# Attention and mixture of experts in one kernel: zero products in the opening, key copies by heads, three weight halves on GpSimd, first tokens in the scores' banks

## The chip, the cores and the metric

The kernel runs on one core of a Trainium2 chip. The metric is the time of one execution in device microseconds (us). The core's engines work side by side and meet through semaphores: TensorE (PE in the profile: matrix products and transposes), VectorE (DVE), ScalarE (ACT), GpSimd (POOL) and SyncE (SP), which issues most DMAs. TensorE writes its results to PSUM, eight banks of 128 x 512 fp32; ScalarE and VectorE read them from there.

## The reference

Block-sparse attention over 4 batches of 8 heads, then a mixture of 16 experts (4 groups of 4) with one expert for each of the 3072 tokens. Cut to what matters:

```python
# attention: S=768, D=64, blocks of 32 keys, window 16
k_sum = k.reshape(B, H, nb, block, D).max(axis=3)
v_sum = v.reshape(B, H, nb, block, D).mean(axis=3)
scores_l = scale * np.matmul(q, k.transpose(0, 1, 3, 2))     # kept where |i - j| < 16
scores_s = scale * np.einsum('bhsd,bhnd->bhsn', q, k_sum) + np.log(block)
a = softmax(concat([where(mask_l, scores_l, -1e9), scores_s]))
x = (a @ concat([v, v_sum])).transpose(0, 2, 1, 3).reshape(B * S, H * D)
# experts: N=3072, D=512, G=4, Eg=4, F=1024
g_idx, g_w = argmax and softmax weight of x @ w_group
e_idx, e_w = argmax and softmax weight of xg @ w_expert[g]
h = np.maximum(xg[mask_e] @ w1[g, e], 0.0)
out[tok_idx] = (g_w * e_w)[:, None] * (h @ w2[g, e])
```

## The kernel before

**Attention.** The 32 heads are done in 16 pairs, each in three steps (g = 0, 1, 2 of query rows). What a step does, and in which order, stands in the table `PLAN`; `START` is the same for the first four steps. The letters: `s` the score products into the scores' banks, `e` VectorE's masked maxima (tiles ss, nm) and ScalarE's exponentials (pr), `t` their transposes, `v` the product with the values and VectorE's division (rs, xt), `m` the block means of the values, `l` the router's logits, `p0` to `p4` the preparation of the next pair. `p0` and `p1` are `put_k` for head 0 and head 1 of the pair: TensorE transposes the head's keys into a bank of `ps_tr` (three banks, in turn), and two copies of 64 rows each, j = 0 and j = 1, put them into the tile kw. `p2` and `p3` do the queries (qt, on ScalarE), and `p4` copies the pads inside kw, takes the block maxima (ks) and copies them in (VectorE). `w` issues four products of zeros (`keep_warm(4)`, 128 x 512 bf16), whose result nobody reads.

**Hand-over.** The function `hook` is called after each step. Around the last ones it begins with the expert that has the most blocks of tokens, called "first": `gather1` fetches two blocks of its tokens (xg) by an indirect DMA from GpSimd, `x_t1` transposes them and splits them into a high and a low half (xT), and `split_w` splits a quarter of the weights w1: ScalarE rounds the high half (w1h), VectorE subtracts it from the weights for the low half (w1l). Products of both halves together have the precision wanted, three for each pair of operands.

**The first expert.** It has four blocks of 128 tokens, done two at a time. Stage 1 (`stage1_2`) makes the hidden layer in four half-blocks jj, 24 products each, each into one bank of the scores; ScalarE then takes the positive part (hTh) and VectorE the low half of that (hTl). During the first pass w2 is split in four parts (w2h, w2l). Stage 2 multiplies with w2. Then come the units (two blocks, one block or small ones) of all experts, one after the other, up to the end.

**Order.** It is fixed when the program is built: each engine executes its instructions in program order. The router's VectorE operations are interleaved by a planner (`Clock`), which sums up estimated times of TensorE and VectorE and puts in router work where VectorE is ahead. Banks are handed out by a ring for each kind (`Banks.next`): "tr" has three banks (63 to 65 in the orders below), "s" three (66 to 68), "av" one (69) and "lg" one (70). When the attention's last steps are built, the third bank of "s" is taken out of its ring and given to "av"; by then two half-blocks of stage 1 have been built.

Of the kernel before, what the change touches and what calls it, by code (L numbers as in the profile page):

```python
# [20 lines left out]
P = 128  # L21
# [29 lines left out]
        ["s", "p3", "l3", "t", "v", "l0", "m0", "e"]]  # L51
START = [["s", "e"], ["s", "m0", "e"], ["s", "w", "t", "m1", "p0", "p1", "e", "p4", "p2", "p3"],
         ["t", "v", "s", "n0", "p0", "p1", "e", "p4"]]
LAG = {"l0": 1, "l1": 2, "l2": 2, "l3": 2}
# [13 lines left out]

XT_AT = 4


# [18 lines left out]
class Clock:  # L90

    pe, dve = float("-inf"), 0.0
    step = 0
# [496 lines left out]
def attention(tc, q, k, v, w_group, w_expert, ident, x_dram, ps, router, hook):  # L590
# [24 lines left out]
    with ExitStack() as st, ExitStack() as nat_st:  # L615
# [125 lines left out]
        def prep(idx, part):  # L741
# [18 lines left out]
            def put_k(h):  # L760
                rows = slice(64 * h, 64 * h + 64)
                out = kw[rows, :, 0:QT].rearrange("p t (r i j) -> p j t r i", i=4, j=2)
                for j, tv in enumerate(tr(kn, h)):
                    (nc.scalar.copy if j == 0 or h and idx in ACT_K1 else V.tensor_copy)(  # L764
                        out=out[:, j], in_=tv.rearrange("p i t r -> p t r i"))
# [121 lines left out]
        for n in range(NG + 3):  # L887
# [4 lines left out]
            for step in START[n] if n < len(START) else PLAN[g]:  # L892
# [10 lines left out]
                elif step[0] == "m" and n < NG:  # L903
                    j = idx + (step == "m0" and n > 2)
                    if (j > 0 or n < 3) and j < len(order):
                        means(j, int(step[1]))
                elif step == "w":
                    keep_warm(4)
                elif step == "n0":
# [36 lines left out]
class Experts:  # L946
# [76 lines left out]
    def split_w(self, row, which, parts, low=True, high=True):  # L1023

        raw = self.raw(row, which)
        for c in parts:
# [9 lines left out]
            if low:  # L1036
                self.V.tensor_tensor(out=l, in0=src, in1=h.bitcast(F32), op=ALU.subtract)

# [7 lines left out]

    def split_t(self, cols, hi, lo, b):

        nc = self.nc
        tp = self.bank("tr", b).rearrange("p (c t) -> p c t", c=4)  # L1050
        for c in range(4):
# [42 lines left out]

    def x_t(self, x, i):
        hi, lo = self.parts(i)
        for half in range(2):
            self.split_t(lambda c: x[half][:, c * P:(c + 1) * P], hi[:, :, half], lo[:, :, half], half)

# [166 lines left out]

    def x_t1(self):
        self.x_t(self.xg1, 0)

# [70 lines left out]
def block_attention_then_moe(tc, q, k, v, w_group, w_expert, w1, w2, out):  # L1340
    nc = tc.nc
    with ExitStack() as st:
# [16 lines left out]
        def hook(n, need, advance, space):  # L1359
# [7 lines left out]
            if n == last - GATHER_AT:  # L1367
                need(2)
                ex.gather1(0)
                ex.load_w(("first", 0), 1, queue=nc.gpsimd)  # L1370
            if n == last - X_AT:
                ex.x_t1()
                if NE > 2:
                    ex.gather1(2)
            for part in range(4):
                if n == last + SPLIT_AT[part] + 1:
                    ex.split_w(("first", 0), 0, [part], high=False)
                if n == last + SPLIT_AT[part]:
# [70 lines left out]
```

## Time and profile before

| | |
|---|---|
| time, median of 3 runs | 515.81 us (514.64 to 517.34) |
| time of the profiled execution | 515.85 us |
| its span, first to last instruction | 514.2 us |
| mean granted TensorE clock | 0.986 |
| TensorE busy | 492.2 us (96%) |
| VectorE busy | 356.6 us (69%) |
| ScalarE busy | 317.8 us (62%) |
| GpSimd busy | 120.9 us (24%) |

The profile is that of one execution. Busy shares are averages over stages with different limits: attention to about 171 us, the first expert to about 236 us, and the units behind it. The granted clock is a share of TensorE's full 2.4 GHz; 0.50 is 1.2 GHz. What ended an engine's idle time stands behind an arrow in the rows, as in "0.45 <-DVE kw".

### The profile page before, as it was taken

How to read it: one execution, taken by the hardware profiler on the slowest of the kernel's cores; microseconds unless marked ns; L12 is line 12 of the kernel's file. 1: busy time of each engine (PE TensorE's matmuls, PEld its weight loads, DVE VectorE, ACT ScalarE, POOL GpSimd, SP SyncE). 2: the span in 40 equal slices, each digit the busy share in tenths (PEclk: the TensorE clock that was granted, in tenths of full speed). 3: DMA queues.
4: the chain of work that ended last, by engine and by line, in shares of the span. 5: the costliest groups of instructions: out<-in, count | busy, mean ns of one | idle time of the engine just before them, and what ended most of it. 6: DMA issues, size and time to landing. Idle time of an engine off the chain costs nothing.

```text
span 514.2 us, 13346 instructions
## 1 busy us (share of the span) xinstructions
PE 492.2 (96%) x4974; PEld 415.5 (81%) x4974; DVE 356.6 (69%) x1084; ACT 317.8 (62%) x597; POOL 120.9 (24%) x205
## 2 busy tenths in 40 slices
PE   8999999999999899999999999999999999999994
PEld 4677767776777698979898989898898989897773
DVE  6687899888977978878755647483836556473773
ACT  5699888888988643216644556473645546474682
POOL 6122112211312600037020203022121202022332
PEclk9799999999999899999999999999999999999998
DMA  9999676879646820069997665665566756754891
GB/s 179 176 181 198 130 168 189 180 155 195 173 113 224 281 90 22 28 220 354 409 403 273 238 229 211 247 225 190 205 211 239 263 212 222 258 191 137 300 359 42
DMA packets 75316, 106.94 MB, mean 208 GB/s; under 512 B 40286, under 2 KB 40366, under 8 KB 75232
## 3 DMA queue, kind: packets, MB, share of 16 engines
q1 hardware_dynamic: 69184, 86.78, 58.5%
q0 software_dynamic: 6048, 19.12, 10.4%
q8 instruction: 43, 0.70, 0.6%
q14 instruction: 41, 0.34, 0.2%
HBM read 97.49 MB, written 13.24 MB: 215 GB/s over the span
## 4 chain that ended last, share of the span: by engine, by line
PE 49%; issue 19%; DMA 12%; DVE 11%; ACT 3%; POOL 3%; POOLq 1%; DVEq 0%; ACTq 0%
PE ps_s L122 26%; DMA out_dram<-y,t_unit_scatter 12%; PE ps_tr L122 12%; PE ps_av L122 10%; DVE ss L795 3%; DVE ks L775 2%; DVE kw L764 1%; ACT kw L764 1%; PE ps_lg L122 1%; POOL ohr L1042 1%; ACT qt L758 1%; PE ps_lg L662 1%; POOLq L1185 1%; ACT pr L804 1%; DVE kw L778 1%
## 5 line engine op out<-in xcount | busy, mean ns | idle before, releaser
L122 DVE TENSOR_TENSOR w2l<-w2r,w2h 128x1024 fp32r<-128x1024 f32 x52 | 63.4, 1225 | 77.1 <-ACT w2h L1035 76.6
L122 PE MATMUL ps_s<-xT,w1h 128*128 128x256 f32 x448 | 83.5, 284 | 0.0
L122 PEld LDWEIGHTS ps_s<-xT,w1h 128*128 128x128 f32 x448 | 70.7, 192 | 1.0 <-issue 0.7
L1082 POOL DMA_INDIRECT out_dram<-y,t_unit_scatter x24 | 25.7, 1069 | 190.9 <-ACT y L1077 97.7
L738 POOL COPY va<-vr 25x256 f32<-25x256 f32 x96 | 35.9, 418 | 118.8 <-DVE vr L735 118.8
L122 PE MATMUL ps_s<-xT,w1l 128*128 128x256 f32 x224 | 63.4, 283 | 0.0
L122 DVE TENSOR_TENSOR w1l<-w1r,w1h 128x1024 fp32r<-128x1024 f32 x52 | 60.4, 1219 | 3.6 <-ACT w1h L1035 3.6
L804 ACT ACTIVATE pr<-ss,nm 128x120 f32<-128x120 f32 x192 | 60.1, 387 | 3.3 <-DVE nm L795 2.9
L1120 ACT ACTIVATE hTh<-ps_s 128x512 fp32r<-128x512 f32 x48 | 28.7, 598 | 53.9 <-PE ps_s L122 31.9
L122 PE MATMUL ps_s<-ohr,w1h 128*128 128x256 f32 x320 | 58.9, 282 | 0.0
L1035 ACT CAST w2h<-w2r 128x1024 fp32r<-128x1024 f32 x52 | 53.8, 1041 | 1.5 <-DVE lg L865 0.9
L1035 ACT CAST w1h<-w1r 128x1024 fp32r<-128x1024 f32 x52 | 50.7, 1051 | 0.4 <-DMA w1r<-in_moe_w_dram 0.4
L122 PEld LDWEIGHTS ps_s<-ohr,w1h 128*128 128x128 f32 x320 | 49.8, 188 | 0.2
L122 DVE SCALAR_TENSOR_TENSOR hTl<-ps_s,hTh 128x512 fp32r<-128x512 f32 x48 | 33.2, 691 | 24.2 <-ACT hTh L1120 21.5
L795 DVE CUSTOM_DVE_ANT_0 ss<-mask,ps_s 128x120 f32<-128x120 f32 x192 | 42.1, 275 | 6.1 <-PE ps_s L122 4.6
L122 PE MATMUL ps_s<-ohr,w1l 128*128 128x256 f32 x160 | 45.0, 281 | 0.0
L122 PEld LDWEIGHTS ps_s<-xT,w1l 128*128 128x128 f32 x224 | 42.9, 192 | 0.3
L122 PE MATMUL ps_s<-kw,qt 64*64 64x120 f32 x768 | 37.5, 282 | 5.7 <-DVE nm L795 4.6
L122 PE MATMUL ps_s<-w2h,hTh 128*128 128x512 f32 x104 | 41.6, 400 | 0.0
L122 PE MATMUL ps_av<-w2h,hTh 128*128 128x512 f32 x104 | 41.6, 400 | 0.0
L122 PE MATMUL ps_av<-w2l,hTh 128*128 128x512 f32 x104 | 41.1, 395 | 0.0
L122 PE MATMUL ps_s<-w2h,hTl 128*128 128x512 f32 x104 | 41.1, 395 | 0.0
(275 smaller groups left out, 1010.6 us busy)
## 6 DMA issues: line engine op xcount, KB each, us to landing
w1r<-in_moe_w_dram SPq DMA_DIRECT2D x30, 1024.0 KB, 8.4
w2r<-in_moe_w_dram SPq DMA_DIRECT2D x28, 1024.0 KB, 5.6
kn<-in_k_dram SPq DMA_DIRECT2D x16, 384.0 KB, 4.5
qn<-in_q_dram SPq DMA_DIRECT2D x16, 384.0 KB, 5.4
va<-in_v_dram SPq DMA_DIRECT2D x32, 192.0 KB, 5.0
x_dram<-xt SPq DMA_DIRECT2D x12, 512.0 KB, 5.4
w2r<-in_moe_w_dram POOLq DMA_DIRECT2D x4, 1024.0 KB
va<-in_v_dram SPq DMA_DIRECT2D x64, 44.0 KB, 4.6
```

The source lines that it names most:

```text
L122: return f(*args, **kw)
L662: nc.tensor.matmul(out=t, lhsT=zero, rhs=zero[:, None, :].broadcast_to([P, 4, P]), start=True, stop=True)
L738: nc.gpsimd.tensor_copy(out=va[KW:NR, i:i + n, :, 0:D], in_=vr[KW:NR].broadcast_to([NBLK + 1, n, 2, D]))
L758: nc.scalar.activation(out=out[:, j], in_=tv.rearrange("p i t r -> p t i r"), func=AF.Copy, scale=-1.0 / 8.0)
L764: (nc.scalar.copy if j == 0 or h and idx in ACT_K1 else V.tensor_copy)(out=out[:, j], in_=tv.rearrange("p i t r -> p t r i"))
L775: V.reduce_max(out=ks, axis=AX.X, in_=kw[:, :, 0:QT].rearrange("p t (a k) -> p t a k", k=BLOCK))
L778: V.tensor_copy(out=kw[:, :, KW:NC], in_=ks[:, None, :].broadcast_to([P, NQT, NBLK]))
L795: V.tensor_tensor_reduce(out=ss[:, u], in0=mask[:, 1 if t == 0 else 2 if t == NQT - 2 else 0], in1=sp[h][:, j], scale=1.0, scalar=3.4e38, ...
L804: nc.scalar.activation(out=pr[:, i, 0:NC], in_=sp[:, i], func=AF.Exp, bias=nm[:, i:i + 1], scale=-1.0)
L1035: self.nc.scalar.copy(out=h, in_=src)
L1082: self.nc.gpsimd.indirect_dma_start(out=self.out, out_offset=bass.IndirectOffsetOnAxis(ap=self.tabs[name, "scatter"][0:y.shape[0], col:col ...
L1120: nc.scalar.activation(out=th[:, js], in_=hp, func=AF.Relu)
```

## The change

It has five parts. (1) The opening's `w` is written `w4`, and two more places issue zero products: `w2` ahead of p3 in step 2 and `w3` ahead of the scores in step 3. (2) `put_k` gives both copies of head 0 to ScalarE and both of head 1 to VectorE, where before each head's first copy went to ScalarE and its second to VectorE. For pairs from 10 on (`ACT_K1`), ScalarE had both copies of head 1; now it has that head's first. (3) Of the first expert's eight low halves three are subtracted by GpSimd: part 2 of w1, parts 1 and 3 of w2. (4) The first token transposes (`x_t1` in `hook`) take banks of "s" instead of "tr". (5) In `hook` the low halves are built ahead of `x_t1` and of the second `gather1`.

```diff
-START = [["s", "e"], ["s", "m0", "e"], ["s", "w", "t", "m1", "p0", "p1", "e", "p4", "p2", "p3"],
-         ["t", "v", "s", "n0", "p0", "p1", "e", "p4"]]
+START = [["s", "e"], ["s", "m0", "e"], ["s", "w4", "t", "m1", "p0", "p1", "e", "p4", "p2", "w2", "p3"],
+         ["t", "v", "w3", "s", "n0", "p0", "p1", "e", "p4"]]
...
+LOW_BY_POOL = ((0, 2), (1, 1), (1, 3))
...
                 for j, tv in enumerate(tr(kn, h)):
-                    (nc.scalar.copy if j == 0 or h and idx in ACT_K1 else V.tensor_copy)(
+                    (nc.scalar.copy if h == 0 or j == 0 and idx in ACT_K1 else V.tensor_copy)(
                         out=out[:, j], in_=tv.rearrange("p i t r -> p t r i"))
...
             if low:
-                self.V.tensor_tensor(out=l, in0=src, in1=h.bitcast(F32), op=ALU.subtract)
+                self.low(row, which, c).tensor_tensor(out=l, in0=src, in1=h.bitcast(F32), op=ALU.subtract)
+
+    def low(self, row, which, c):
+        return self.nc.gpsimd if row[0] == "first" and (which, c) in LOW_BY_POOL else self.V
...
-    def split_t(self, cols, hi, lo, b):
+    def split_t(self, cols, hi, lo, b, bank="tr"):
 
         nc = self.nc
-        tp = self.bank("tr", b).rearrange("p (c t) -> p c t", c=4)
+        tp = self.bank(bank, b).rearrange("p (c t) -> p c t", c=4)
...
+            for part in range(4):
+                if n == last + SPLIT_AT[part] + 1:
+                    ex.split_w(("first", 0), 0, [part], high=False)
             if n == last - X_AT:
-                ex.x_t1()
+                ex.x_t1("s")
                 if NE > 2:
                     ex.gather1(2)
             for part in range(4):
-                if n == last + SPLIT_AT[part] + 1:
-                    ex.split_w(("first", 0), 0, [part], high=False)
                 if n == last + SPLIT_AT[part]:
                     ex.split_w(("first", 0), 0, [part], low=False)
```

What stands in a row of VectorE in the middle of the attention, between the maxima of one step and the pads of kw, before:

```order
L764 COPY kw_135<-ps_tr_63 64x12x32
L848 COPY xT<-ps_tr_64 128x256
L826 RECIPROCAL rs<-ps_av_69 128x4
L827 TENSOR_TENSOR xt_113<-ps_av_69,rs 128x2x128
L764 COPY kw_135<-ps_tr_63 64x12x32
L772 COPY kw_135<-kw_135 128x11x16
```

and of the changed kernel, at the same place (its lines from 762 on are counted one higher):

```order
L849 COPY xT<-ps_tr_64 128x256
L827 RECIPROCAL rs<-ps_av_69 128x4
L828 TENSOR_TENSOR xt_113<-ps_av_69,rs 128x2x128
L765 COPY kw_135<-ps_tr_63 64x12x32 x2
L773 COPY kw_135<-kw_135 128x11x16
```

The copy of head 0 that stood ahead of the division by rs is gone from here, and two copies of head 1 stand behind it.

ScalarE in stage 1 of the first expert's first pass; `hTh` is the positive part of a half-block, read from the bank named behind the arrow. Before (the fourth reads ps_s_67):

```order
L1120 ACTIVATE hTh_3102<-ps_s_66 128x512
L848 COPY xT<-ps_tr_65 128x256
L861 COPY lT<-ps_lg_70 128x192
L1120 ACTIVATE hTh_3102<-ps_s_67 128x512
L1035 CAST w2h_3483<-w2r_3096 128x1024 x2
L1120 ACTIVATE hTh_3102<-ps_s_66 128x512
```

and now:

```order
L1124 ACTIVATE hTh_3107<-ps_s_68 128x512
L849 COPY xT<-ps_tr_63 128x256
L862 COPY lT<-ps_lg_70 128x192
L1124 ACTIVATE hTh_3107<-ps_s_66 128x512
L1036 CAST w2h_3488<-w2r_3101 128x1024 x2
L1124 ACTIVATE hTh_3107<-ps_s_66 128x512
L1036 CAST w2h_3488<-w2r_3101 128x1024 x2
L1124 ACTIVATE hTh_3107<-ps_s_67 128x512
```

The second and the third half-block, jj = 1 and 2, now use the same bank, 66; VectorE's hTl read the same banks in the same order.

TensorE behind the last product of stage 1 of the second pass, where stage 2 of the third block begins; `ps_lg<-ohr,bo_unit` are products that build the table of the units' tokens. Before:

```order
L122 MATMUL ps_av_69<-w2h_3483,hTh_3102 128x512
L122 MATMUL ps_av_69<-w2l_3484,hTh_3102 128x512
L122 MATMUL ps_av_69<-w2h_3483,hTl_3103 128x512
L122 MATMUL ps_av_69<-w2h_3483,hTh_3102 128x512
L122 MATMUL ps_av_69<-w2l_3484,hTh_3102 128x512
L122 MATMUL ps_av_69<-w2h_3483,hTl_3103 128x512
L122 MATMUL ps_lg_70<-ohr,bo_unit 62x128 x6
```

and now:

```order
L123 MATMUL ps_lg_70<-ohr,bo_unit 62x128 x18
L123 MATMUL ps_av_69<-w2h_3488,hTh_3107 128x512
L123 MATMUL ps_av_69<-w2l_3489,hTh_3107 128x512
L123 MATMUL ps_av_69<-w2h_3488,hTl_3108 128x512
L123 MATMUL ps_av_69<-w2h_3488,hTh_3107 128x512
L123 MATMUL ps_av_69<-w2l_3489,hTh_3107 128x512
L123 MATMUL ps_av_69<-w2h_3488,hTl_3108 128x512
L123 MATMUL ps_lg_70<-ohr,bo_unit 62x128 x6
```

18 of the 24 products moved ahead of stage 2, and six behind its first six; before, the other 18 came six matmuls later. The 24 products of `bo_unit` with ohr that follow, behind one product of the look-up (ps_lg of ident and look), stand behind six w2 matmuls after it before the change and behind twelve now.

## Rows read from the trace of the kernel before

**Rows 1.** The page, granted TensorE clock in 40 slices, tenths of full speed.

```profile
PEclk9799999999999899999999999999999999999998
```

**Rows 2.** Windows, columns: stretch, length; busy us of each engine; clock, DMA share, GB/s.

```profile
19.00:25.50 6.50, 6.35 (x70) 4.98 (x70) 3.58 (x15) 3.42 (x9) 0.00 (x0) 0.50 1.26 194
...
30.54:164.11 133.57, 126.60 (x2164) 98.29 (x2158) 113.81 (x582) 117.21 (x298) 28.34 (x78) 1.00 0.79 177
...
176.00:179.00 3.00, 3.00 (x36) 2.54 (x34) 2.96 (x8) 0.54 (x1) 0.61 (x1) 0.50 0.84 277
...
179.00:180.00 1.00, 1.00 (x13) 0.56 (x12) 0.90 (x6) 0.00 (x0) 0.00 (x0) 0.79 1.01 383
...
230.00:470.00 240.00, 240.00 (x1558) 216.86 (x1557) 143.08 (x155) 128.86 (x166) 50.88 (x45) 1.00 0.69 249
```

**Rows 3.** Waits of TensorE from 30 to 170 us.

```profile
PE ps_s L122 <- DVE nm L795: 4.0, 12, 1.0
```

**Rows 4.** Timeline of the opening: start, us, engine, line, operation, idle before.

```profile
12.69 1.04 PE L662 MATMUL ps_lg<-zero 128*128 128x512 bf16 x4
...
16.16 0.55 PE L122 MATMUL ps_tr<-ident,qn 96*128 96x96 f32 x4 [0.45 <-DVE kw L764]
...
18.70 0.39 PE L122 MATMUL ps_s<-kw,qt 64*64 64x120 f32 x2 [0.63 <-DVE kw L778]
...
19.24 0.66 PE L122 MATMUL ps_s<-kw,qt 64*64 64x120 f32 x5 [0.15 <-ACT qt L758]
...
30.54 0.29 DVE L731 COPY vp<-ps_tr 128x128 f32<-128x128 f32 x1 [0.83 <-ACT pr L804]
```

**Rows 5.** The tile kw, ScalarE's key copies: min, median and max ns.

```profile
L764 ACT COPY kw<-ps_tr x38: 480/503/512, 5.5 to 156.3; 64x384 f32<-64x384 f32 x38
```

**Rows 6.** Timeline of one pair of heads in the attention.

```profile
41.77 0.56 DVE L764 COPY kw<-ps_tr 64x384 f32<-64x384 f32 x1
...
43.53 0.56 DVE L764 COPY kw<-ps_tr 64x384 f32<-64x384 f32 x1 [0.19 <-ACT kw L764]
...
44.12 0.26 DVE L772 COPY kw<-kw 128x176 f32<-128x176 f32 x1
...
41.78 0.69 PE L122 MATMUL ps_av<-va,ptS 121*64 121x65 f32 x16
```

**Rows 7.** Timeline of the hand-over and of stage 1's half-block 1.

```profile
172.89 0.89 PE L122 MATMUL ps_tr<-identr,xg 128*128 128x128 f32 x8 [0.69 <-DVE sc_first L122]
...
175.22 0.70 PE L122 MATMUL ps_tr<-ident,pr 128*121 128x128 f32 x4 [1.20 <-DVE xT L122]
...
175.68 1.22 DVE L122 TENSOR_TENSOR w1l<-w_first,w1h 128x1024 fp32r<-128x1024 f32 x1
...
176.81 0.42 DVE L848 COPY xT<-ps_tr 128x256 f32<-128x256 f32 x1
...
188.19 0.40 PE L122 MATMUL ps_s<-xT,w1h 128*128 128x256 f32 x2
...
188.51 0.60 ACT L1120 ACTIVATE hTh<-ps_s 128x512 fp32r<-128x512 f32 x1 [1.28 <-PE ps_s L122]
...
189.79 0.68 DVE L122 SCALAR_TENSOR_TENSOR hTl<-ps_s,hTh 128x512 fp32r<-128x512 f32 x1
```

**Rows 8.** GpSimd: its copies of va, and the last six on the timeline.

```profile
L738 POOL COPY va<-vr x96: 394/399/1447, 15.0 to 173.4; 25x256 f32<-25x256 f32 x96
...
170.64 3.18 POOL L738 COPY va<-vr 25x256 f32<-25x256 f32 x6 [1.08 <-DVE vr L735]
```

**Rows 9.** Timeline of TensorE at the building of the units' tables.

```profile
221.16 1.08 PE L122 MATMUL ps_lg<-ohr,bo_unit 128*62 128x128 f32 x12
...
222.78 0.58 PE L122 MATMUL ps_lg<-ohr,bo_unit 128*62 128x128 f32 x6 [0.53 <-DVE bo_unit L122]
...
226.45 1.72 PE L122 MATMUL ps_lg<-bo_unit,ohr 128*128 128x124 f32 x12
...
228.35 1.80 PE L122 MATMUL ps_lg<-bo_unit,ohr 128*128 128x124 f32 x12 [0.18 <-DVE bo_unit L122]
```

More of the change, by code (lines that the diff above doesn't have):

```diff
@@ L906, in attention @@
                         means(j, int(step[1]))
-                elif step == "w":
-                    keep_warm(4)
+                elif step[0] == "w":
+                    keep_warm(int(step[1]))
                 elif step == "n0":
@@ L1093, in parts, with x_t @@
         return [self.xT2[i % 2][:, m] for m in range(2)]
-    def x_t(self, x, i):
+    def x_t(self, x, i, bank="tr"):
         hi, lo = self.parts(i)
         for half in range(2):
-            self.split_t(lambda c: x[half][:, c * P:(c + 1) * P], hi[:, :, half], lo[:, :, half], half)
+            self.split_t(lambda c: x[half][:, c * P:(c + 1) * P], hi[:, :, half], lo[:, :, half], half, bank)
     def x_t2(self, i):
@@ L1265, in gather1, with x_t1 @@
             self.gather(("first", i + half), self.xg1[half])
-    def x_t1(self):
-        self.x_t(self.xg1, 0)
+    def x_t1(self, bank="tr"):
+        self.x_t(self.xg1, 0, bank)
     def first(self):
```

## The prediction

> **What bounds the kernel now.** I read the page first, then the waits by stage, then the timelines where the edits are. TensorE's granted clock falls below nine tenths of full speed in three of the page's 40 slices, the second, the fourteenth and the last [rows 1]. Three regimes follow. From 230 to 470 us TensorE is busy every microsecond [rows 2]: nothing the change does there counts, and whatever arrives at 230 us earlier or later ends earlier or later by as much. In the attention (30 to 170 us) the bound alternates: in 12 places, 4.0 us together, the score matmuls wait for VectorE's maxima [rows 3], so lateness on VectorE passes into TensorE, in part. In the opening and at the hand-over to the first expert (172 to 180 us) the clock halves: 0.50 from 19.0 to 25.5 and from 176 to 179 us, 0.79 in the microsecond after [rows 2]. In front of each fall TensorE had stood still: 0.45, 0.63 and 0.15 us before 19.24 [rows 4], 0.69 and 1.20 us before 176 [rows 7].
>
> **The sum is made against the profiled execution**, 515.85 us (span 514.2 and 1.65 around it), practically the median of the runs, 515.81. What this kernel's measurement can tell from no change is about 0.5%, 2.6 us.
>
> **Opening, five more zero products.** Four took 1.04 us, 0.26 each [rows 4]. Two stand ahead of the last query transposes, where TensorE waits 0.45 us (copied keys release a bank); three ahead of the scores of step 3, where it waits 0.63 us. 5 x 0.26 = 1.3 us fill some 1.2 us of waiting; the scores' own rest waits until 19.24 for the query copies on ScalarE, so the 0.1 us too much costs nothing; without that cover the five cost 1.3 us. If the clock then stays up, the 6.35 us that TensorE is busy from 19.0 to 25.5 [rows 2] would need 3.2. The stage can't shrink that far: VectorE (3.58 busy of the 6.50) and ScalarE (3.42) hand results back and forth. Of VectorE's 2.92 us of standing I take 1.85 as gone: vp of pair 2 moves from 30.54 [rows 4] to 28.7. Bounds: 0 (the clock falls all the same, since at full speed TensorE has less to do in that stretch) and 2.9.
> **-1.85.**
>
> **Key copies by heads.** The numbers of copies don't change; ScalarE's take 0.50 us [rows 5] and VectorE's 0.56 [rows 6]. The two copies of one head run one after the other; those of different heads need not wait for each other. Before, VectorE did one copy of head 0 in a slot in which it would wait for the values (41.77, while TensorE's value product ends at 41.78 + 0.69 = 42.47) and one of head 1 at 43.53; the step behind (the pads' copy) began at 44.12 [rows 6]. Now both of VectorE's stand behind xt, the second one's slot ahead of the values is empty. With xt drawn to its own gate (the value product, 42.47): xt 42.72 to 43.06, then two copies 0.59 apart, pads at 44.24: 0.12 later. The same reckoning for all pairs: 0.12 in four of them, 0.29 and 0.58 in the two where the values come late, about -0.4 in one where ScalarE's chain was the later one and its exponentials now start earlier, within 0.14 or nothing in the others: 0.8 together. As TensorE waits for VectorE in 12 places only, I take 0.6. Bounds: -0.5 (only the gains pass on) and +2 (every lateness passes on, and ScalarE's two copies in a row hold its exponentials too).
> **+0.6.**
>
> **Hand-over.** One w1l half leaves VectorE, 1.13 us from its start to the next [rows 7], and the first token transposes go into the scores' banks, so they need not wait 0.69 us for a bank, nor the probability transposes 1.20 us for theirs [rows 7]. VectorE's queue gains 1.13, TensorE at most 1.89; I take 1.4 up to the end of half-block 1 of stage 1. But the bank ring turns against it. The orders in the section on the change show VectorE reading half-blocks 0 to 3 of stage 1 from banks 68, 66, 66, 67, where it was 66, 67, 66, 67: the two extra turns move the ring by two, and one of its three tiles is taken out after half-block 1. So half-block 2 may not begin until both engines have read half-block 1. Before: the two matmuls from 188.19 are the last of half-block 1 and, some 0.1 us on, the first of half-block 2, which goes on at once; ScalarE reads at 188.51, VectorE, busy with the router, at 189.79 for 0.68 [rows 7]. After, all 1.4 earlier: TensorE done at 186.9, VectorE at 188.39 + 0.68 = 189.07, next matmul 189.1: a new wait of 2.2, and the 1.4 gained become 189.1 - 188.3 =
> **+0.8.** Bounds: -1.4 (VectorE reads at once) and +2.3.
>
> **The clock behind that wait.** 2.2 us without a matmul is more than the 1.23 and 1.89 us of standing that preceded the two falls of before. I count a third fall of the size of the second: 3 us at 0.50 and one at 0.79 [rows 2], worth 1.5 + 0.2 in a stretch that TensorE bounds.
> **+1.7.** Bounds: 0 and 3.3 (half of the 6.5 us of the first fall).
>
> **GpSimd's three halves.** No row shows a subtraction on GpSimd. VectorE does one in 1.22 us [rows 7], which bounds it from below. GpSimd's copies of 256 columns with one input take 0.40 [rows 8]; four times the columns and two inputs give 3.2, the upper bound. The work is nearest to that kind of copy, so I take 2.5. The Trainium skill's GPSIMD Engine Reference (section 3.1) gives 4497 ns for a tensor_tensor on 2048 columns against VectorE's 2293, so an estimate of 2.25 us for 1024; by it the sum is the same. The w1 half then runs behind the copies that end at 170.64 + 3.18 = 173.82 [rows 8], to 176.4, and is read by half-block 2 at 188 or later; the two w2 halves follow ScalarE's casts in half-blocks 2 and 3 and are read in stage 2, behind part 0. At any value up to 3.2 all three are hidden; behind the first, two token gathers start 2.5 us later, and their tokens are wanted only behind stage 1. If this cover were gone each would cost its excess.
> **0.**
>
> **The router behind it.** Two w2l halves less give VectorE 2.4 us, and the planner moves router operations up. The products that build the units' tables are placed by it: before, TensorE waits 0.53 and 0.18 us there and its 24 last ones take 1.72 + 1.80 us at the pace of VectorE's eight products, where 12 of another kind took 1.08 [rows 9], so some 1.2 of their 3.5 is waiting that looks busy. In the new order (section on the change) 18 products stand ahead of stage 2 of the third block rather than six behind its first six matmuls, and the 24 stand behind six matmuls more than before. I count 0.7 + 1.2 = 1.9 won and 0.4 lost by the 18, which come earlier than their VectorE inputs.
> **-1.5.** Bounds: -2.6 and +0.7.
>
> **Sum:** -1.85 + 0.6 + 0.8 + 1.7 + 0 - 1.5 = -0.25: 515.85 - 0.25 = **515.6 us**: the opening's gain and the router's are spent at the new wait and on the clock behind it.
>
> **Rivals.**
> 1. *The wait is there but the clock does not fall behind it:* -0.25 - 1.7 = -1.95, 513.9. For it: a wait of 1.0 us in the attention [rows 3] brought no fall, its clock stays at 1.00 [rows 2]; against: 2.2 is twice that.
> 2. *VectorE reads half-block 1 in time and no wait arises* (the planner's router operations ahead of it start earlier than I moved them): -1.85 + 0.6 - 1.4 - 1.5 = -4.15, 511.7. Against it: ScalarE's read and VectorE's, 0.6 + 0.68, follow each other, so at least 1.3 us of waiting is left before the next matmul.
> 3. *The zero products do nothing, the clock falls at the same place or soon after:* -0.25 + 1.85 = +1.6, 517.5. For it: at full speed TensorE stands in 19 to 25.5 about half the time.
> 4. *The key copies' lateness passes on in every pair* (the other side): at 0.58 us, as in the pair with late values, times 13 pairs, 7.5 us in place of 0.6: 522.5. It is slower by over 2.6 us from 0.26 us a pair on. Against it: in most pairs the slot that was filled is now merely empty, and the gate is the value product.
> 5. *GpSimd's subtraction holds VectorE up:* for the first, 2.5 us of VectorE's queue in the hand-over, 515.6 + 2.5 = 518.1. No row shows the two engines with two-input work side by side. The GPSIMD Engine Reference of the Trainium skill (section 1) says that GpSimd shares its SBUF interface with VectorE, with contention when VectorE has two SBUF inputs; by that rule, VectorE's subtraction of the next w1 half would be the one to suffer.
>
> **Chances.** Forecast 0.42 (its own range 514.5 to 516.8, where the opening gives 0.9 to 2.9); rival 1 0.20; rival 2 0.12; rival 3 0.14; rival 4 0.06; rival 5 0.06. Faster by over 0.5% (below 513.2): rival 2, half of rival 1 (an opening or a router gain at its bound) and a tenth of the forecast's 0.42, in which several terms lie at their good ends: 0.12 + 0.10 + 0.05 = 0.27, and 0.03 for key copies better than zero: 0.30. Slower (above 518.4): rival 4, half of 5, a fifth of 3 and 0.03 of the forecast: 0.15. The rest, 0.55, within. The range from rival 2 to rival 5's end: 511.8 to 518.2.
>
> **What the profile after would show.** Opening right: clock 1.00 between 19 and 25, vp of pair 2 near 28.7. Key copies: pads' copy about 0.1 later after the scores of a pair, vp spacing 9.8. Hand-over: a wait of TensorE of about 2.3 us, released by VectorE's hTl, after half-block 1; clock 0.50 for some 3 us behind it. GpSimd: three subtractions of 2 to 3 us, nobody waiting for them. Router: the 24 products without waits. Wrong would be: no such wait; a clock that falls in the opening; vp spacing that shrinks by tenths in most pairs, which would carry the time below 513.

## The result, and the profile after

The changed kernel takes 519.06 us in the median of 18 runs, the kernel before 515.80 in the median of 20 runs beside them; two more runs of the changed kernel, of 764.92 and 1150.25 us, are far from all others and left out here and in the ratio. The ratio of the two is 1.0052, 95% interval 1.0035 to 1.0069: slower by half a per cent, 2.7 us. The forecast was 515.6 with a range of 511.8 to 518.2, so the time lies above the range. The profiled execution took 518.14 us, 2.3 more than that of before.

The page of the changed kernel (busy time of the engines, granted clock), to set against [rows 1]:

```profile
PE 487.9 (94%) x4979; PEld 412.7 (80%) x4979; DVE 357.5 (69%) x1081; ACT 319.3 (62%) x597; POOL 131.5 (25%) x208
...
PEclk9999999999999999999999999999999999999998
```

and its windows, against [rows 2]:

```profile
19.00:25.50 6.50, 5.41 (x99) 3.98 (x101) 4.81 (x23) 4.61 (x12) 0.00 (x0) 1.00 1.26 194
...
176.00:179.00 3.00, 2.78 (x38) 2.43 (x39) 2.83 (x11) 0.18 (x1) 2.54 (x3) 1.00 0.84 326
...
230.00:470.00 240.00, 240.00 (x1560) 217.00 (x1559) 142.94 (x155) 129.08 (x166) 51.03 (x45) 1.00 0.69 249
```

The clock is at full speed in this execution, in the opening, at the hand-over and behind it: on that score it had every advantage, and it is slower all the same. The time went into TensorE's waits. The attention (30 to 170 us), against the 4.0 us in 12 places of [rows 3], and the hand-over with the stretch behind it (176 to 236 us):

```profile
PE ps_s L123 <- DVE nm L796: 7.8, 13, 1.3
...
PE ps_s L123 <- DVE hTl L123: 2.1, 1, 2.1
PE ps_av L123 <- DVE xt L828: 1.7, 2, 1.2
PE ps_lg L123 <- DVE bo_unit L123: 1.0, 2, 0.5
```

and the last of these rows before the change:

```profile
PE ps_lg L122 <- DVE bo_unit L122: 0.7, 2, 0.5
```

The first row is the key copies' lateness, the second the wait on bank 66 that the prediction gave 2.2 us, and the last the wait at the units' tables, which the prediction counted as won and which has grown. One pair of the attention, the same place as [rows 6]:

```profile
38.99 0.29 DVE L732 COPY vp<-ps_tr 128x128 f32<-128x128 f32 x1 [0.83 <-ACT pr L805]
41.22 0.18 DVE L827 RECIPROCAL rs<-ps_av 128x4 f32<-128x4 f32 x1 [0.53 <-PE ps_av L123]
41.89 1.13 DVE L765 COPY kw<-ps_tr 64x384 f32<-64x384 f32 x2
43.05 0.26 DVE L773 COPY kw<-kw 128x176 f32<-128x176 f32 x1
...
45.25 0.64 PE L123 MATMUL ps_s<-kw,qt 64*64 64x120 f32 x14 [0.46 <-DVE nm L796]
```

and the same scores before:

```profile
46.31 0.64 PE L122 MATMUL ps_s<-kw,qt 64*64 64x120 f32 x14 [0.24 <-DVE nm L795]
```

VectorE now stands 0.53 us where the copy of head 0 was, has both copies of head 1 behind xt, and the pads' copy begins 4.06 us behind vp. TensorE's scores wait 0.46 us for the maxima; before, 0.24. The hand-over, beside [rows 7]:

```profile
176.22 0.69 PE L123 MATMUL ps_av<-va,ptS 121*64 121x65 f32 x16 [1.19 <-DVE xt L828]
177.30 0.38 PE L123 MATMUL ps_s<-xT,w1h 128*128 128x256 f32 x1
188.80 0.39 PE L123 MATMUL ps_s<-xT,w1h 128*128 128x256 f32 x1 [2.07 <-DVE hTl L123]
...
186.77 0.60 ACT L1124 ACTIVATE hTh<-ps_s 128x512 fp32r<-128x512 f32 x1 [1.26 <-PE ps_s L123]
...
188.06 0.68 DVE L123 SCALAR_TENSOR_TENSOR hTl<-ps_s,hTh 128x512 fp32r<-128x512 f32 x1
```

Stage 1 begins at 177.30, and after its half-block 1 TensorE stands 2.07 us until VectorE has read the bank: 188.06 + 0.68 = 188.74, next product at 188.80. Then what no row of before could show, GpSimd's subtractions of w2 and VectorE beside them:

```profile
190.43 2.44 POOL L1038 TENSOR_TENSOR w2l<-w2r,w2h 128x1024 fp32r<-128x1024 f32 x1 [10.64 <-ACT w2h L1036]
194.53 3.42 POOL L1038 TENSOR_TENSOR w2l<-w2r,w2h 128x1024 fp32r<-128x1024 f32 x1 [1.67 <-ACT w2h L1036]
...
190.52 0.27 DVE L123 TENSOR_REDUCE mx<-lg 128x30 f32<-128x120 f32 x1
190.83 2.18 DVE L123 TENSOR_TENSOR dd<-lg,mx 128x120 f32<-128x120 f32 x1
193.04 0.28 DVE L123 SCALAR_TENSOR_TENSOR c<-dd,iom 128x120 f32<-128x120 f32 x1
...
194.48 1.22 DVE L123 TENSOR_TENSOR w2l<-w2r,w2h 128x1024 fp32r<-128x1024 f32 x1
195.61 2.46 DVE L123 TENSOR_TENSOR eoh<-c 128x96 f32<-128x96 f32 x1
```

GpSimd subtracts from 190.43 to 192.87. VectorE's reduction of one input (mx) beside it takes its usual 0.27 us; the subtraction dd, of two inputs, takes 2.18 and ends at 193.01, just behind GpSimd's; c, when GpSimd is idle again, takes 0.28. In the second place it goes both ways: VectorE's own w2l comes first (194.48 to 195.70) and GpSimd's, begun at 194.53, takes 3.42 instead of 2.44; then VectorE's eoh, 2.46 us, ends at 198.07 behind GpSimd's end at 197.95.

What this costs TensorE in this kernel is nothing that the trace shows. From its first product behind the wait to the end of stage 1 it is busy all the time:

```profile
188.80:219.20 30.40, 30.40 (x218) 27.81 (x219) 26.65 (x96) 9.37 (x15) 7.89 (x4) 1.00 0.13 44
```

Last the 24 products of `bo_unit` with ohr, beside [rows 9], and the VectorE operations that feed them:

```profile
226.90 1.45 PE L123 MATMUL ps_lg<-bo_unit,ohr 128*128 128x124 f32 x12
228.77 1.79 PE L123 MATMUL ps_lg<-bo_unit,ohr 128*128 128x124 f32 x12 [0.42 <-DVE bo_unit L123]
...
224.38 1.91 DVE L123 TENSOR_TENSOR bo_unit<-eq_unit,w_all 128x372 fp32r<-128x372 f32 x4
227.72 1.91 DVE L123 TENSOR_TENSOR bo_unit<-eq_unit,w_all 128x372 fp32r<-128x372 f32 x4 [1.43 <-PE ps_lg L123]
```

and VectorE's before:

```profile
225.32 3.89 DVE L122 TENSOR_TENSOR bo_unit<-eq_unit,w_all 128x372 fp32r<-128x372 f32 x8
```

VectorE is earlier, but stops after four of its eight operations and waits 1.43 us for TensorE: the kernel keeps two tiles of bo_unit (`bufs=2`), each filled by two operations and read by six products.

Both traces by marks. Each number is the difference of two start times in the timelines; vp 2 is the copy vp of pair 2, jj 0 the first product of stage 1, hTh k ScalarE's read of half-block k, y the first unit result behind 230 us, and the end the moment at which the issue of the last scatter is over.

| | vp 2 | to vp 13 | to vp 15 | to jj 0 | to hTh 1 | to hTh 2 | to hTh 7 | to y | to last hTh | to end |
|---|---|---|---|---|---|---|---|---|---|---|
| before | 30.54 | 111.52 | 22.04 | 15.54 | 8.87 | 3.41 | 26.23 | 18.43 | 261.20 | 12.55 |
| after | 29.02 | 112.90 | 22.02 | 13.37 | 9.46 | 5.21 | 26.76 | 18.26 | 261.16 | 14.06 |

Up to the units the two profiled executions differ by 0.42 us only; 1.5 us more is in the last column, and the rest of their difference behind it. The 0.53 us from hTh 2 to hTh 7 are no time of TensorE's: before, ScalarE read half-block 2 late, behind two casts, now it waits for it:

```profile
191.93 0.59 ACT L1120 ACTIVATE hTh<-ps_s 128x512 fp32r<-128x512 f32 x1
...
191.98 0.60 ACT L1124 ACTIVATE hTh<-ps_s 128x512 fp32r<-128x512 f32 x1 [1.68 <-PE ps_s L123]
```

So beside the marks above some of TensorE's own starts are used below: hb 2, the first product of half-block 2, and, behind the last product of stage 1, the first product behind the tables.

### The profile page after: what moved, and what is told of

Same layout as the page of the kernel before. It is cut to its first block, busy times and chain, and to the rows that moved or that the text cites. A ratio compares the mean times of both kernels' runs of the same rounds, so it can differ in the third digit from the quotient of the medians.

```text
span 516.6 us, 13404 instructions
## 1 busy us (share of the span) xinstructions
PE 487.9 (94%) x4979; PEld 412.7 (80%) x4979; DVE 357.5 (69%) x1081; ACT 319.3 (62%) x597; POOL 131.5 (25%) x208
## 4 chain that ended last, share of the span: by engine, by line
PE 77%; DVE 15%; DMA 2%; issue 2%; ACT 1%; SPq 1%; POOL 0%; POOLq 0%; ACTq 0%; DVEq 0%
PE ps_s L123 46%; PE ps_av L123 17%; PE ps_tr L123 12%; DVE kw L765 3%; DVE ks L776 2%; DVE ss L796 2%; DMA kn<-in_k_dram 2%; PE ps_lg L123 1%; DMA out_dram<-y,t_unit_scatter 1%; ACT pr L805 1%; DVE kw L779 1%; DVE kw L773 1%; PE ps_lg L663 1%; SPq L648 1%; DVE xt L828 1%
## 5 line engine op out<-in xcount | busy, mean ns | idle before, releaser
L123 DVE TENSOR_TENSOR w2l<-w2r,w2h 128x1024 fp32r<-128x1024 f32 x50 | 61.1, 1225 | 77.5 <-ACT w2h L1036 77.0
L1086 POOL DMA_INDIRECT out_dram<-y,t_unit_scatter x24 | 25.5, 1061 | 194.5 <-ACT y L1081 111.0
L739 POOL COPY va<-vr 25x256 f32<-25x256 f32 x96 | 34.8, 407 | 118.6 <-DVE vr L736 117.6
```

The costliest lines, as they stand in the source:

```text
L123: return f(*args, **kw)
L739: nc.gpsimd.tensor_copy(out=va[KW:NR, i:i + n, :, 0:D], in_=vr[KW:NR].broadcast_to([NBLK + 1, n, 2, D]))
L1086: self.nc.gpsimd.indirect_dma_start(out=self.out, out_offset=bass.IndirectOffsetOnAxis(ap=self.tabs[name, "scatter"][0:y.shape[0], col:col ...
```

## The experiments

16 experiments were run on four chips; a ratio is always against the kernel before on the same chip. Its median differs by 2.2 us between the chips (515.66 to 517.89), the executions of one kernel on one chip by up to 6 us, with mean granted clocks from 0.979 to 0.999, so the marks of the profiles carry the argument and the times check it.

**Again.** The changed kernel (e1_again), and later the kernel before (e10_before_again), unedited.

> The changed kernel once more, nothing edited, for a second profile. Theory A (the loss sits in the body of the program: new wait of 2.07 us behind half-block 1 of stage 1, key copies 0.23 us a pair, and a clock that falls in some executions): the marks repeat, vp of pair 2 at 29.0, of pair 13 at 141.9, the wait 2.1 us, the eighth hTh at 218.7, within 0.1 where the clock stays at 1.00; time near 518.7. Theory B (the loss of the first profile is the end: its last scatter began at 511.34 where it was 509.45 before, while the units ran only 0.42 late): the end moves by 1 to 2 us from profile to profile with the body fixed, in either direction.

> The kernel before, nothing edited, for a second profile. Z1: the granted clock of 19 to 26 us differs from execution to execution; if it is 1.00 here, vp of pair 2 comes by 29.5 without any zero product added. Z2: 0.5 again, vp of pair 2 at 30.5. The end, from the last hTh to the last scatter's landing, 12.0 to 12.6 us as in the profiles without a subtraction on GpSimd, if that is what sets it, or up to 14.6 if it is chance.

e1: 519.81 us, ratio 1.0044 (1.0025 to 1.0064). The marks repeat (vp 2 at 29.47, then 112.87, 22.00, 13.36, 9.38), with one new thing: from hTh 1 to hTh 2 it takes 6.68 us, not 5.21. Windows of e1 behind the wait:

```profile
188.00:190.00 2.00, 0.91 (x4) 0.91 (x5) 1.33 (x4) 1.41 (x2) 0.00 (x0) 0.80 0.00 0
190.00:193.00 3.00, 3.00 (x18) 3.00 (x17) 2.97 (x3) 0.58 (x1) 2.28 (x1) 0.57 0.00 0
```

and the product that waited, in its timeline:

```profile
189.09 0.51 PE L123 MATMUL ps_s<-xT,w1h 128*128 128x256 f32 x1 [2.05 <-DVE hTl L123]
```

That is the fall of the clock that the prediction gave 1.7 us; it costs 6.68 - 5.21 = 1.47. It came in three of the four profiles that have the wait (e1, and e3 and e12 below), and not in the one shown first. The kernel before, second profile, 518.89 us:

```profile
19.00:26.00 7.00, 6.23 (x83) 4.50 (x82) 4.01 (x16) 3.88 (x10) 0.00 (x0) 0.62 1.26 185
26.00:30.00 4.00, 4.00 (x50) 3.27 (x50) 3.77 (x19) 3.84 (x11) 0.36 (x1) 0.82 1.18 218
176.00:180.00 4.00, 2.69 (x44) 2.26 (x48) 3.97 (x9) 1.80 (x3) 1.36 (x2) 1.00 0.84 299
```

The opening's fall comes later, and vp 2 at 32.23, but most of that is from before the fall: vp of pair 0 comes at 13.96 (12.25 in the first profile), and from there to vp 2 it takes 18.27 us (18.29). At the hand-over the clock does not fall at all, and vp 15 to jj 0 takes 14.50, not 15.54; by hTh 1 half of that is made up, 23.84 against 24.41. So the fall at the hand-over is a matter of one execution, and worth 0.6 us there. From the last hTh to the end it takes 14.38: theory B is right that the end moves without any edit. The 18 profiles of this study fall into two sorts there, 12.0 to 12.7 us in seven and 14.0 to 14.8 in eleven, and four of the five kernels that were profiled twice show one value of each: before 12.55 and 14.38, the zero products alone (e7 and e11) 12.24 and 14.77, e5 and e14 14.62 and 12.12, e9 and e13 14.72 and 12.63. What differs is above all how long GpSimd waits ahead of the last scatter (3.02 us in the first profile of the kernel before, 4.70 in the second); why is not shown. Nor is it shown that the change has no part in it: all seven profiles of kernels in which GpSimd subtracts w2 lie in the upper sort, and four of the other eleven.

**The ring set back (e2_ring) and the old key copies (e3_oldkeys), alone and together (e4_ring_oldkeys).**

```diff
                 ex.x_t1("s")
+                ps["s"].n -= 2
```

```diff
-                    (nc.scalar.copy if h == 0 or j == 0 and idx in ACT_K1 else V.tensor_copy)(
+                    (nc.scalar.copy if j == 0 or h and idx in ACT_K1 else V.tensor_copy)(
```

> The changed kernel with the scores' bank ring set back by the two turns that the first token transposes took, so that half-blocks 0 to 3 use 66, 67, 66, 67 again. Theory A: the wait of 2.07 us is gone, half-block 2 starts at about 186.7 instead of 188.8, stage 2 and the units 1.5 to 2.1 us earlier; 1.7 us less than the changed kernel, about 517.0. Theory C (VectorE's router work bounds this stretch anyhow, as its lateness was only uncovered by the ring): the wait goes but the units begin less than 0.5 us earlier, since TensorE waits for the tables' inputs instead.

> The changed kernel with the key copies as before (first copy of a head on ScalarE, second on VectorE). Theory A: the pairs return to 9.74 us from 9.97, vp of pair 13 comes 1.35 us earlier, at about 140.5, and everything behind shifts by as much: 517.3. Rival: the pairs' lateness is made up at the hand-over, where ScalarE and the last values wait for one another; the first product of stage 1 then moves by less than 0.5 us and the time stays near 518.7.

> Both edits, ring set back and key copies as before; what stays are the zero products, GpSimd's three halves and the transposes in the scores' banks. Theory A: the two gains add, 1.7 + 1.35 = 3.0 less than the changed kernel and some 0.6 to 1 less than before the change: about 515.4 at a clock of 1.00 throughout. Theory B (the end decides): no better than before, 516 to 518.

Ratios 1.0007 (0.9984 to 1.0030), 1.0012 (0.9989 to 1.0036) and 0.9987 (0.9967 to 1.0008), beside 1.0044 for e1 on the same chip: 518.28, 518.94 and 517.36 us against its 519.81. The key copies: vp 2 to vp 13 takes 111.50 and 111.49 us in e3 and e4, 112.88 in e2: 1.37 us, and TensorE's waits for the maxima in e3 are those of [rows 3] again, 4.0 in 12 places. Nothing of it is made up at the hand-over (13.36 and 13.37 in e3 and e2); the rival of e3 is out. The times of e3 and e4 stayed 1.6 and 2.0 us above what was expected. The ring: hTh 1 to hTh 2 takes 3.41 us in e2 and e4, as before, so wait and clock fall go with the bank. But theory C was right in part: from hTh 2 to hTh 7 it takes 28.05 and 28.06 us, 1.8 more than before the change, and a wait for another thing stands there. TensorE, VectorE and GpSimd in e2:

```profile
198.53 0.50 PE L123 MATMUL ps_av<-w2l,hTh 128*128 128x512 f32 x1 [1.57 <-DVE w2l L123]
...
191.52 2.19 DVE L123 TENSOR_TENSOR dd<-lg,mx 128x120 f32<-128x120 f32 x1
193.75 2.36 DVE L123 SCALAR_TENSOR_TENSOR c<-dd,iom 128x120 f32<-128x120 f32 x1
...
191.13 4.84 POOL L1038 TENSOR_TENSOR w2l<-w2r,w2h 128x1024 fp32r<-128x1024 f32 x2 [11.84 <-ACT w2h L1036]
```

GpSimd's two subtractions follow each other, 191.13 to 195.97; VectorE's dd and c, 0.28 us each elsewhere, fill the same stretch. VectorE's own w2l comes late by it and TensorE waits 1.57 us for it. That is not router work in general but these two operations. VectorE's order in this stretch is the same as in the changed kernel; there the wait on the bank keeps TensorE back by more than that, which hides it.

**GpSimd's halves taken away: only w1's left (e5_pool_w1_only), none (e6_no_pool), copies in place of the w2 subtractions (e8_pool_copies), one w2 half (e15_one_w2_half).** All with the ring set back and the old key copies. The first edit is e5's; e6 has `()` there and e15 `((0, 2), (1, 3))`; the second is e8's.

```diff
-LOW_BY_POOL = ((0, 2), (1, 1), (1, 3))
+LOW_BY_POOL = ((0, 2),)
```

```diff
+                if which == 1 and self.low(row, which, c) is not self.V:
+                    self.nc.gpsimd.tensor_copy(out=l, in_=src)
+                else:
```

> The kernel with the ring set back and the old key copies, and of GpSimd's three halves only the one of w1 (the two of w2 go back to VectorE). Theory L (VectorE's operations with two inputs from SBUF stand still while GpSimd subtracts: dd took 2.19 us and the operation behind it 2.36 where each took 0.28 before): both take 0.28 again, the wait of TensorE of 1.6 us for w2l goes, and from the first product of stage 1 to the eighth hTh it takes 39.2 us or less instead of 40.85; 1.6 us less in all, 515.8 where that kernel took 517.4, and under the kernel before by 0.3%. Rival Q (those spans are VectorE waiting its turn for ScalarE's dd or for inputs, not for GpSimd): the spans stay, and VectorE with 2.4 us more to do is later still.

> The same with none of the halves on GpSimd. Both theories: the hand-over is 1 us later than with the w1 half on GpSimd, as VectorE has 1.2 us more ahead of the last values: from vp of the last pair to the first product of stage 1 about 14.4 us instead of 13.4; behind it as with the w1 half alone. Theory L: still faster than with all three by 0.6 us; rival Q: slower than it by 1 us or more.

> The kernel with the ring set back and the old key copies, where GpSimd copies parts 1 and 3 of w2 in place of subtracting the high half: it reads one input, so the low halves hold other numbers than they should. Theory L in its narrow form (GpSimd's second input stream is what shuts VectorE out): VectorE's dd and c take 0.28 us while GpSimd copies. Theory L in its wide form (any GpSimd operation on SBUF of that size): they take as long as GpSimd's copy, 1 to 1.7 us.

> Ring set back, old key copies, zero products in; of w2 only part 3 on GpSimd, besides the w1 half. If VectorE and GpSimd exclude one another in operations with two inputs from SBUF: one operation of VectorE, not two, is drawn out to about 2.4 us, or GpSimd's subtraction is drawn out by VectorE's; from the third hTh to the eighth between 26.2 (no w2 half) and 28.05 us (two). If it is not the exclusion: both as with two halves.

e5: 516.24 us, ratio 1.0006 (0.9985 to 1.0027); e6: 516.04, 1.0012 (0.9995 to 1.0029). hTh 2 to hTh 7 takes 26.24 and 26.23 us, as before the change, where e4 took 28.06: theory L, 1.8 us. VectorE in e5 has two more halves and is not late, so rival Q is out:

```profile
195.64 0.27 DVE L123 TENSOR_REDUCE mx<-lg 128x30 f32<-128x120 f32 x1
195.94 0.28 DVE L123 TENSOR_TENSOR dd<-lg,mx 128x120 f32<-128x120 f32 x1
196.26 0.28 DVE L123 SCALAR_TENSOR_TENSOR c<-dd,iom 128x120 f32<-128x120 f32 x1
```

Their times do not show it: against the kernel before they are no better than e4, and the 0.3% that was expected of e5 did not come. On that chip the kernel before ran at a mean clock of 0.9925 where it had 0.9880 on the chip of e4; that this is the reason is not shown. With one w2 half (e15, one profiled execution of 519.00 us) exactly one operation of VectorE is drawn out:

```profile
192.74 2.18 DVE L123 TENSOR_TENSOR dd<-lg,mx 128x120 f32<-128x120 f32 x1
194.96 0.28 DVE L123 SCALAR_TENSOR_TENSOR c<-dd,iom 128x120 f32<-128x120 f32 x1
...
191.86 2.92 POOL L1038 TENSOR_TENSOR w2l<-w2r,w2h 128x1024 fp32r<-128x1024 f32 x1 [14.43 <-PE ps_tr L123]
```

and among TensorE's waits:

```profile
PE ps_tr L123 <- DVE eb L123: 1.9, 1, 1.9
```

The number of drawn-out operations goes with the number of halves, but the price does not, and the expectation of 26.2 to 28.05 us missed: it takes 29.78. In its order VectorE's eb comes behind the drawn-out operation, and TensorE's rank products, which read eb, ahead of the rest; TensorE waits 1.9 us for it, and the clock falls behind that wait (0.68 in 200 to 204 us). With copies in e8 the low halves hold the full weights. GpSimd's two copies, one input each, and VectorE:

```profile
189.02 2.02 POOL L1039 CAST w2l<-w2r 128x1024 fp32r<-128x1024 f32 x2 [9.99 <-DVE lg L866]
...
190.03 2.08 DVE L123 TENSOR_TENSOR w2l<-w2r,w2h 128x1024 fp32r<-128x1024 f32 x1 [0.64 <-ACT w2h L1036]
192.34 0.28 DVE L123 TENSOR_TENSOR dd<-lg,mx 128x120 f32<-128x120 f32 x1
```

dd is free, having come after them, but VectorE's w2l takes 2.08 us, 0.86 more than its 1.22, and begins while GpSimd copies (to 191.04). So this one operation speaks for the wide form: GpSimd's one-input copy too keeps a two-input operation of VectorE waiting. As dd met no copy, the narrow form's test at that operation did not come about. e8 settles something else: VectorE has the same order in it, from stage 1 to the tables, as in e4, nothing but GpSimd's two instructions differs, and from hTh 2 to hTh 7 it takes 26.22 us against 28.06. So the 1.8 us come from GpSimd's subtractions and not from the planner's order.

The w1 half holds nothing up. While GpSimd subtracts it in the changed kernel, VectorE makes the low halves xT, one input of which is in PSUM; two of them take 1.29 us, and 1.28 elsewhere:

```profile
173.91 2.36 POOL L1038 TENSOR_TENSOR w1l<-w_first,w1h 128x1024 fp32r<-128x1024 f32 x1
...
173.91 1.29 DVE L123 TENSOR_TENSOR xT<-ps_s,xT 128x512 fp32r<-128x512 f32 x2 [0.41 <-ACT xT L1058]
```

What it wins at the hand-over differs from execution to execution: behind vp 15, jj 0 comes after 14.29 us without that half (e6), with it after 13.36 or 13.37 in eight profiles and after 13.72 to 14.06 in four (e5, e8, e13, e15), though e5 and e14 are one kernel, and so are e9 and e13.

**The zero products: alone (e7_zero_only, e11_zero_again: the kernel before with the change's `START`), and taken out (the edit below).** e12_after_no_zero is the changed kernel without them; e9_no_zero and e13_no_zero_again are e5 without them, e14_zero_again is e5 again, and e16_no_zero_no_pool is e6 without them.

```diff
-START = [["s", "e"], ["s", "m0", "e"], ["s", "w4", "t", "m1", "p0", "p1", "e", "p4", "p2", "w2", "p3"],
-         ["t", "v", "w3", "s", "n0", "p0", "p1", "e", "p4"]]
+START = [["s", "e"], ["s", "m0", "e"], ["s", "w4", "t", "m1", "p0", "p1", "e", "p4", "p2", "p3"],
+         ["t", "v", "s", "n0", "p0", "p1", "e", "p4"]]
```

> The kernel before with the five zero products alone. Theory A: the clock stays at 1.00 from 19 to 26 us, vp of pair 2 comes at 28.9 to 29.8 instead of 30.5, and the pairs behind keep 9.74 us; all of it is kept up to the end: 1.0 to 1.5 us, 0.2 to 0.3%. Rival: the hand-over's own clock fall and waits take it back, the first product of stage 1 moves by less than 0.4 us.

> The kernel before with the zero products alone, once more, with more runs: six runs gave 0.42% more than the kernel before, while the profile showed everything up to the units 0.8 us earlier. Z1: 0.1 to 0.4% slower again, with a mean clock no better than that of the kernel before. Z2: 0.2% faster.

> Ring set back, old key copies, only the w1 half on GpSimd, and the five zero products taken out too: what is left of the change are the first token transposes in the scores' banks, the w1 half on GpSimd and the order in the hook. Theory Z1 (the zero products pay only in executions whose clock would fall in the opening; at an equal clock they cost): about 0.5 to 1 us less than with them, 515.0, and below the kernel before by 0.1 to 0.3%. Theory Z2 (they win 1.3 us, as the first profiles show): 1.3 us more than with them, 517.3.

> The changed kernel without its five new zero products. Z1: 0.5 to 1 us less than the changed kernel, at most the same: 518 to 519. Z2: 1.3 us more than the changed kernel, near 520.

> Ring set back, old key copies, the w1 half on GpSimd, no new zero products: timed again beside the same with them. If the zero products pay by keeping the clock up: slower than the kernel with them by 0.5 to 1.2 us. If what they win in the mean is spent at an equal clock: the same within 0.5 us, and 0.2 to 0.3% under the kernel before.

> The same with the five zero products. If they pay: 0.3 to 0.5% under the kernel before on this chip, mean clock 0.994 against 0.990. If not: 0.1 to 0.3% under it.

> Ring set back, old key copies, no half on GpSimd, no new zero products: only the first token transposes in the scores' banks and the order in the hook are left of the change. The hand-over from vp of the last pair to the first product of stage 1 takes 14.3 us, as in the kernel with zero products and without GpSimd, against 13.4 to 14.1 with the w1 half on GpSimd; so 0.3 to 0.9 us slower than e13, and 0.1 to 0.2% under the kernel before.

In all 12 profiles of kernels with the five products the granted clock of 19 to 26 us is 1.00; of the six without them it is 0.51, 0.62 and 0.51 in three (before, e10, e16) and 1.00 in three (e9, e12, e13). So, as far as 18 profiles tell, they hold the clock, and theory Z2's mistake is to take the fall of [rows 2] as the rule. From vp of pair 0 to vp 2 it takes 18.27 to 18.30 us in the three with the fall, 17.04 to 17.31 in the three without it, and 16.6 to 17.7, 17.1 in the mean, in the twelve with the products: they win what the fall costs, 1.1 us, and nothing where it would not have come. The times go both ways: e7 1.0042 (1.0025 to 1.0058, six runs), the same kernel as e11 0.9986 (0.9969 to 1.0002); e12, the changed kernel without them, 1.0050 (1.0030 to 1.0070), as slow as with them, and above the 518 to 519 us of Z1, on a chip on which the kernel before takes 517.89. e16 came out 1.0 us behind e13 in the median, and not 0.1 to 0.2% under the kernel before; in its profile the clock fell in the opening, at the hand-over and behind the tables. Side by side on one chip, with the rest mended:

| kernel | median us | ratio | mean clock of its runs |
|---|---|---|---|
| e14, with the products | 513.94 | 0.9974 (0.9951 to 0.9998) | 0.9965 |
| e13, without | 515.01 | 0.9997 (0.9977 to 1.0016) | 0.9929 |
| e16, without, and no half on GpSimd | 516.01 | 1.0004 (0.9985 to 1.0023) | 0.9915 |
| before | 515.66 | | 0.9933 |

e14 beats both kernels here, the one before by 0.26%; the same kernel had 1.0006 as e5, and e9, the same as e13, had 0.9975 (0.9952 to 0.9998), each on another chip. The mean clock also counts the end of a run, where it is below full speed in every profile, so it does not measure the opening alone. So the mended version is level with the kernel before or a little under it, and clearly under the changed one. The intervals of e13 and e14 overlap, so what the products are worth in the mean (1.1 us by these medians) stays open.

## Why the prediction was wrong

Term by term, in the prediction's order, read from the starts of the instructions. The first column is what the prediction counted; "before" is the profile that it was made against, e10 the second profile of the same kernel.

| term, and the stretch it is read from | forecast | before | e10 | after | after - before |
|---|---|---|---|---|---|
| opening: up to vp 2 | -1.85 | 30.54 | 32.23 | 29.02 | -1.52 |
| key copies: vp 2 to vp 15 | +0.6 | 133.56 | 133.60 | 134.92 | +1.36 |
| hand-over with its wait: vp 15 to hb 2 | +0.8 | 24.21 | 23.64 | 24.86 | +0.65 |
| clock behind the wait, GpSimd's halves: hb 2 to the last product of stage 1 | +1.7, 0 | 29.52 | 29.52 | 29.63 | +0.11 |
| router: from there to the first product behind the tables | -1.5 | 12.15 | 12.13 | 11.98 | -0.17 |

**The step that failed: "The router behind it", -1.5; measured -0.17.** The prediction took TensorE to be held up at the units' tables by VectorE's lateness, so that an earlier VectorE would take the waiting away. VectorE did come earlier: its first operation on bo_unit with the weights (w_all) starts 5.95 us behind the last product of stage 1, where it was 7.48. But the tables did not follow. VectorE fills two tiles of bo_unit and then waits for TensorE to read one, 1.43 us; TensorE waits 0.42 for the third tile where it waited 0.18, and its 24 products take 3.50 us up to the next one, 3.53 before. The other wait, 0.53, only moved, with the 18 products, ahead of stage 2. The 1.2 us of "waiting that looks busy" were too much besides: twelve of these products whose inputs were ready took 1.45, so of 3.5 some 0.6 could be won. That GpSimd's hold on VectorE was not the reason is shown by e8, where it drew out nothing but one w2l: the stretch takes 12.05 us there, 11.97 to 11.99 in the seven profiles with subtractions of w2 on GpSimd, and 12.13 to 12.15 in the ten without.

**Key copies, +0.6, mis-sized: the second failure.** 1.37 us were measured by vp 13 (112.87 to 112.92 against 111.49 to 111.57 in all 18 profiles). The mechanism and the place were right. In the four like pairs 0.12 was worked out for the pads' copy, and it came 0.22 later (4.06 us behind vp, 3.84 before): the first copy began 0.45 us behind xt's start (41.44 to 41.89), where 0.34 was reckoned. And the pairs grew by 0.23, 9.74 to 9.97 us, so all of it passed on. Both 0.12 and the choice of 0.6 out of 0.8, as if lateness passed on in part, were too small.

**GpSimd's three halves, 0: right in the time, by luck.** The spans were sized well (2.36 to 2.44 against 2.5), but "all three are hidden" left out what they do to VectorE. It was to be freed of 2.4 us, and stood for 1.9 and 2.2, the time by which dd and eoh were drawn out. This cost nothing here because the wait on the bank had just set TensorE back: e3 and e4 differ in the ring alone, and TensorE waits 2.05 us for hTl and never for w2l in e3, and 1.56 us for w2l in e4, where the stretch grows by 1.8 us. Rival 5 named the mechanism, but put it at the w1 half, beside which VectorE's longer operations (the low halves xT) read from PSUM, and gave it 0.06. The rule of the Trainium skill's GPSIMD Engine Reference (section 1), cited there, is borne out by the traces: the operation of one input (mx, 0.27) passes, that of two (dd, 2.18) waits.

**Hand-over, +0.8, right (+0.65).** The wait was 2.07 (2.2 forecast), released by hTl, behind half-block 1. Part of the agreement is luck: against e10, where no fall of the clock stands at the hand-over, 1.0 us was gained by hTh 1 (23.84 to 22.83) instead of 1.4, and the net is +1.2.

**The clock behind that wait, +1.7, right in most executions.** About 1.5 us in three of four profiles, nothing in the one profiled first (rival 1).

**Opening, -1.85, right in mechanism and oversized.** 1.52 by vp 2 against an execution in which the clock fell; the kernel before keeps its clock in part of its executions (some of them have a mean of 0.997 or 0.998, and 6.5 us at 0.50 alone take 0.006 from it), and its median contains those.

**The end.** 1.5 of the 2.3 us between the two profiled executions lie between the last hTh and the end of the last scatter's issue; no step counted on them, and the kernel before alone shows a difference as large (12.55 and 14.38).

Against e10, with a clock of 1.00 from the hand-over on and without the end, the change costs 1.32 (keys) + 1.22 (hand-over with its wait) + 0.11 - 0.15 (router) = 2.5; with the fall behind the wait, 4.0; less what the zero products save where the clock would have fallen. The measured 2.7 lies between; how often each fall comes is not known.

## What to carry to other kernels

When one engine seems to pace another, count the tiles between them: with two tiles, VectorE's earlier start at the tables was worth a tenth of what was counted on. Before work is moved to GpSimd, look at what VectorE does in the same microseconds: if those are operations with two inputs from SBUF, the work is not moved but put in VectorE's way. When a change takes turns from a ring of banks, write down which bank each later user gets, up to the place where the ring's length changes. And take a clock fall or an end seen in one profile as one draw: the second profile of the unchanged kernel shows one of its two falls gone and its end 1.8 us longer.

## What the runs showed of the hardware

In these traces GpSimd and VectorE exclude each other in operations on SBUF where VectorE reads two inputs: VectorE's dd (128 x 120) took 2.18 us beside GpSimd's 2.44 us subtraction and 0.28 without one (e5), and GpSimd's took 3.42 us behind a 1.22 us one of VectorE. A GpSimd copy with one input (about 1 us) held VectorE's two-input subtraction once too, 2.08 instead of 1.22, while VectorE's reduction beside a subtraction of GpSimd kept its 0.27, and two of its subtractions with one input from PSUM took 1.29 beside one, 1.28 elsewhere. GpSimd's subtraction of 128 x 1024 takes 2.36 to 2.44 us undisturbed, twice VectorE's 1.22. And the granted clock of one and the same program differs between executions: the kernel before has 0.50 from 19.0 to 25.5 us and from 176 to 179 in one profile, and 0.62 from 19 to 26, 0.82 from 26 to 30 and 1.00 from 176 to 180 in the next.
